# Fused attention and two MoE-style layers on one core: layer 2's weights split into two parts before they are parked in DRAM

## Chip, cores, metric

One core of one Trainium2 chip (trn2). The metric is the device time of one launch in microseconds (us). Three runs of the kernel before took 1051.81, 1053.36 and 1053.62 us: the median is 1053.36.

## What is computed

```python
def _moe_ref(x, w_in, w_out):            # layer 1
    h = x @ w_in
    g = h * np.clip(h + 3.0, 0.0, 6.0) / 6.0
    return (g @ w_out).astype(np.float32)

def _moe2_ref(x, w_in, w_out):           # layer 2
    h = x @ w_in
    sp = np.where(h > 20.0, h, np.log1p(np.exp(np.minimum(h, 20.0))))
    g = h * np.tanh(sp)
    return (g @ w_out).astype(np.float32)

attn_out = _attn_ref(q, k, v)            # 4 batches, 8 heads, 576 tokens, head size 64
x = attn_out.transpose(0, 2, 1, 3).reshape(2304, 512)
x = _moe_ref(x, moe_w_in, moe_w_out)     # 512 -> 2048 -> 512
return _moe2_ref(x, moe2_w_in, moe2_w_out)
```

Weights come as float64. The change touches only how layer 2's weights get from their float64 form to the operands of the matmuls.

## The kernel before

The 2304 tokens are cut into five blocks `j` (four of 512 columns, the last of 256), the 2048 hidden units into 16 tiles `f` of 128. One **step** is a triple (layer `m`, block `j`, tile `f`); there are 160: steps 0 to 79 are layer 1 (16 to a block, so steps 64 to 79 are its short block), steps 80 to 159 layer 2. In a step TensorE (PE) computes `ff_in` (L257 to L259: 4 x 3 matmuls of x and W_in into the PSUM tile `h`), the other engines apply the activation, and some steps later PE computes `ff_out` (L755 to L757: 4 x 3 matmuls into `y`). Three matmuls for one product, since each operand is a pair of rounded float32 tiles, an upper part and the rest: `xh`, `xl` for x, `wh`, `wl` for the weights, `gh`, `gl` for the activation. `gh` is a copy with rounding on ScalarE (ACT, L331), `gl` a subtraction on GpSimd (POOL, L338). `ff_out` of step n needs `gl` of step n at its second matmul, L756.

The order on every engine is written out by hand: for each step n, `MOE_PLAN` lists the stages in order, each with the lag in steps at which it runs. There are three plans: for layer 1's first block, for the rest of layer 1, and for layer 2. In the second plan a step issues, as far as the change and the prediction touch it: `w0` to `w3` and `whi`, `wlo` (the six pieces of a weight conversion), `in` of step n, `out` of step n - 2, `xa`, `xm`, `xh`, `xl` (the four pieces by which a tile of the next block's x is made), `c3`, `gh` and `gl` of step n - 1, `dma`, and last `a` (the first activation of step n). Engines run in their own order and wait for each other by semaphores; all these DMAs are issued on SyncE's queue (SP) in program order, and one that waits holds up those behind it.

**Conversion of layer 2's weights.** In steps 16 to 47 one half tile (128x512) a step is converted from float64 bits: `fetch2` (L145) loads the raw bits a step ahead, then `narrow` makes the float32 number: `w0` ACT `m<-raw` (L157), `w1` POOL `v<-raw` (L162), `w2` and `w3` two VectorE (DVE) operations on the bits (L165, L168). `narrow2` stores the number `v` to the DRAM tile `w2d` (L856) in the next step. In the DVE's order `w2` of step n stands ahead of `c3` of step n - 1 (L313), and POOL's `w1` of step n ahead of `gl` of step n - 1.

**x tiles in those steps.** Steps 22, 26, 28, 30 and again 38, 42, 44, 46 each also make one of the four x tiles of the next block: POOL adds two loaded parts (`xa`, L227), DVE multiplies (`xm`, L232), ACT rounds (`xh`, L239), DVE subtracts (`xl`, L244). Their loads (`load_x`, L214 to L217) are issued in steps 21, 22, 25, 28 and 37, 38, 41, 44. The part `xs` has a single buffer, so its load waits for the `xa` before.

**Loading back.** A weight tile of layer 1 is used last in its short block. `reload2` (L805) then loads `w2d[f]` into the tile `wl`, issued in step 70 + f and held until PE's `ff_out` of step 64 + f has released the tiles. Three steps later `resplit2` turns it into the pair: ACT copies it with rounding into `wh` (L810, 128x1024), then POOL and DVE each subtract one half in place (L814). These are the stages `r1` and `r2`, in steps 73 to 88; layer 2 begins at step 80.

Of the kernel before, what the change touches and what calls it, by code (L numbers as in the profile page):

```python
# [18 lines left out]
P = 128  # L19
# [6 lines left out]
FT = DFF // P  # L26
# [33 lines left out]
MOE_PLAN = (  # L60
    (
        ("c3", 1), ("gh", 1), ("gl", 1), ("w2", 0), ("w3", 0), ("w0", 0), ("xa", 0), ("w1", 0),
        ("xm", 0), ("in", 0), ("dma", 0), ("a", 0), ("out", 2), ("xh", 0), ("xl", 0), ("r2", 0),
        ("whi", 0), ("r1", 0), ("wlo", 0), ("evac", 3),
    ),
    (
        ("w0", 0), ("in", 0), ("w1", 0), ("out", 2), ("r1", 0), ("xa", 0), ("xm", 0), ("w2", 0),
        ("c3", 1), ("dma", 0), ("gh", 1), ("w3", 0), ("r2", 0), ("gl", 1), ("xh", 0), ("xl", 0),
        ("whi", 0), ("evac", 3), ("wlo", 0), ("a", 0),
    ),  # L70
    (
# [24 lines left out]
    (15.16, "gl", 0), (15.2, "conv", 3, 1, 6), (15.67, "in", 3),  # L96
)
AHEAD = 6
RELOAD = 6
RESPLIT = 3  # L100
XLOAD = (-11, -10, -7, -4), (-11, -9, -9, -6)
XSPLIT = (-10, -6, -4, -2), (-10, -8, -7, -1)
END = 0
# [2 lines left out]
def f32(ap):  # L106
    return ap.bitcast(F32)
# [7 lines left out]
def fused_kernel(ctx: ExitStack, tc: tile.TileContext, qT, kT, vv, w1, w2, outT):  # L115
    nc = tc.nc
# [6 lines left out]
    xr = ctx.enter_context(tc.tile_pool(name="xr", bufs=2))  # L123
    dpool = ctx.enter_context(tc.tile_pool(name="dpool", bufs=1, space=DRAM))
# [6 lines left out]
    x1d = dpool.tile([KT, 2, P, NT], F32, tag="x1d", name="x1d")  # L131
    rsd = dpool.tile([KT, 2, NT], F32, tag="rsd", name="rsd")
    x2d = dpool.tile([KT, P, NT], F32, tag="x2d", name="x2d")
    w2d = dpool.tile([FT, P, 1024], F32, tag="w2d", name="w2d")

    raws = {}

# [10 lines left out]
    def narrow(raw, name, x=None, tag="val", pool=False):  # L148

        low, high = raw[:, :, 0], raw[:, :, 1]  # L150
        x = x or wst.tile([P, 512], F32, tag="q", name=f"b{name}")


        if pool:
            nc.gpsimd.tensor_scalar(x, high.bitcast(F32), REBASE, 1.0, op0=ALU.mult, op1=ALU.mult)
        else:
            nc.scalar.activation(x, high.bitcast(F32), AF.Copy, scale=REBASE)  # L157
        yield

# [182 lines left out]
    with ExitStack() as late:  # L342
# [416 lines left out]
    def spare():  # L759
        return m4.tile([P, 512], F32, tag="o", name=f"m{now[0]}")  # L760
# [27 lines left out]


    conv, dmas, stores = {}, {}, {}  # L790
    xs, res = ({}, {}, {}, {}), ({}, {})

    def narrow2(n):
        for val in narrow(raws.pop((1, n)), f"2_{n}", spare(), ("q", "val")[n % 2]):
            yield
        yield
        f, c = divmod(n, 2)
        store(now[0] + 1, w2d[f, :, 512 * c:512 * c + 512], val)

    def fetch2(n):  # L800
        raws[1, n] = fetch(w2, *divmod(n, 2))

    def reload2(f):

        nc.sync.dma_start(f32(weight_tiles(1, f)[1]), w2d[f])  # L805

    def resplit2(f, t):
        hi, lo = wt[1, f]
        if t == 0:
            nc.scalar.activation(hi, f32(lo), AF.Copy)  # L810
        else:
            for c, eng in enumerate((nc.gpsimd, nc.vector)):
                cs = slice(512 * c, 512 * c + 512)
                eng.tensor_sub(lo[:, cs], f32(lo[:, cs]), f32(hi[:, cs]))  # L814

    for n, (m, j, f) in enumerate(steps):
        if m == 0 and j == 0 and f >= WMID:
            for c in range(2):
                put(conv, n - 3, weights1_spare, f, c)
                put(dmas, max(n - AHEAD, 0), fetch1, f, c, True)  # L820
        if m == 0 and 1 <= j <= 2:
            i = (j - 1) * FT + f
            put(dmas, n - 1, fetch2, i)
            put(conv, n, narrow2, i)
        if (m, j) == (0, NJ - 1):
            put(dmas, n + RELOAD, reload2, f)
            put(res[0], n + RELOAD + RESPLIT, resplit2, f, 0)
            put(res[1], n + RELOAD + RESPLIT, resplit2, f, 1)
        if f == 0 and n:
            for k in range(KT):  # L830
                put(dmas, n + XLOAD[m][k], load_x, m, j, k)
                i = n + XSPLIT[m][k]
                put(xs[0], i, add_x, m, j, k)
                put(xs[3], i, mul_x, m, j, k)
                put(xs[1], i, split_x, m, j, k, 0)
# [15 lines left out]
    def calls(*ds):  # L851
        def run_stage(n, m):
            if m == group(n):
                for d in ds:
                    for fn, *args in d.pop(n, ()):
                        fn(*args)  # L856
        return run_stage


    def conv_step(i):  # L860
        def run_stage(n, m):
            if m != group(n):
                return
            if i == 0:
                active[n] = [fn(*args) for fn, *args in conv.pop(n, ())]
            for x in active.get(n - 1 if m == 0 and i >= 2 else n, ()):
                next(x, None)
        return run_stage

    stages = dict(  # L870
        a=stage(act_a), b1=stage(act_b1), b2=stage(act_b2), ln=stage(act_ln),
        rexp=stage(act_rexp), mul=stage(act_mul), c1=stage(act_c1), c2=stage(act_c2),
        c3=stage(act_c3), gh=stage(act_gh), gl=stage(act_gl), evac=stage(evacuate),
        out=stage(ff_out), dma=calls(stores, dmas), xa=calls(xs[0]), xh=calls(xs[1]), xl=calls(xs[2]), xm=calls(xs[3]),
        r1=calls(res[0]), r2=calls(res[1]),
        w0=conv_step(0), w1=conv_step(1), w2=conv_step(2), w3=conv_step(3),
        whi=conv_step(4), wlo=conv_step(5),
    )
    stages["in"] = stage(ff_in)
    for n in range(len(steps) + 6):  # L880
        now[0] = n
        for i, plan in enumerate(MOE_PLAN):
            for name, lag in plan:
                if (name, n - lag) not in begun:
                    stages[name](n - lag, i)
    assert not (dmas or stores or conv or any(xs) or any(res))


# [37 lines left out]
```

## Time and profile before

| | us |
|---|---|
| runs, median of three | 1053.36 |
| the profiled execution's own time | 1053.55 |
| its span, first to last instruction | 1051.5 |
| PE busy | 998.3 (95%) |
| DVE busy | 647.0 (62%) |
| POOL busy | 548.8 (52%) |
| ACT busy | 515.3 (49%) |

The span is the time between the first and last instruction; 2.05 us lie around it. Busy shares are averages over stages with different limits. In the page's 40 slices (26.3 us each) PE is below nine tenths in two places, slices 9 to 12 (layer 1's start) and 25 to 28 (layer 2's start). Mean granted clock of TensorE is 0.99 of full speed.

### The profile page before, as it was taken

The page shows a single profiled execution, that of the slowest core. Times are in us where ns is not written, and L with a number is a line of the kernel's source. Part 1 is how long each engine was busy: PE and PEld are TensorE (multiplying, and loading weights), DVE is VectorE, ACT ScalarE, POOL GpSimd, SP SyncE. Part 2 cuts the span into 40 slices and gives each one's busy share as a digit, 9 for nine tenths or more (in the row PEclk, how much of TensorE's full clock was granted, in tenths as well). Part 3 has the DMA queues.
Part 4 walks back from the last instruction along what each step waited for, and adds up shares of the span by engine and source line. Part 5 has one row for each costly group of instructions (what it writes and reads, how often), then busy time and mean ns, then how long its engine had stood idle before and what let it go on. Part 6 is the DMA issues. An engine that isn't in the chain of part 4 may idle for free.

```text
span 1051.5 us, 14665 instructions
## 1 busy us (share of the span) xinstructions
PE 998.3 (95%) x5184; PEld 843.5 (80%) x5184; DVE 647.0 (62%) x1055; ACT 515.3 (49%) x1159; POOL 548.8 (52%) x494
## 2 busy tenths in 40 slices
PE   6999999988879999999999998889999999999997
PEld 5898898866557888888888996568888888888897
DVE  6888878778974444444222247996665666565664
ACT  4788888754433333333222354454444444444454
POOL 6555544567653443434222274655565555555644
PEclk9999999999999999999999999999999999999999
DMA  6677678595214755753200362000100100010010
GB/s 174 173 204 198 169 183 217 187 337 191 74 60 154 227 187 169 234 172 100 70 20 11 128 213 100 9 13 1 60 21 1 61 11 11 1 55 6 1 41 21
DMA packets 88729, 112.11 MB, mean 107 GB/s; under 512 B 41552, under 2 KB 53840, under 8 KB 88656
## 3 DMA queue, kind: packets, MB, share of 16 engines
q1 hardware_dynamic: 88656, 111.18, 34.4%
q8 instruction: 40, 0.66, 0.3%
q14 instruction: 33, 0.27, 0.1%
HBM read 74.97 MB, written 27.34 MB: 97 GB/s over the span
## 4 chain that ended last, share of the span: by engine, by line
PE 69%; POOL 8%; issue 8%; DVE 7%; ACT 4%; DMA 3%; SPq 1%; POOLq 0%; ACTq 0%; DVEq 0%
PE y L756 10%; PE y L757 10%; PE y L755 10%; PE h L259 10%; PE h L258 10%; PE h L257 10%; PE o L588 3%; POOL gl L338 3%; PE t L558 2%; PE s L485 2%; DVE v L168 2%; ACT p L518 2%; POOL wl L814 1%; DMA qb<-qs 1%; PE s L486 1%
## 5 line engine op out<-in xcount | busy, mean ns | idle before, releaser
L756 PE MATMUL y<-gl,wh 128*128 128x512 f32 (+1 forms) x640 | 238.8, 373 | 17.4 <-POOL gl L338 17.3
L257 PE MATMUL h<-xh,wh 128*128 128x512 f32 (+1 forms) x640 | 238.9, 373 | 9.7 <-ACT wh L185 6.9
L259 PE MATMUL h<-xh,wl 128*128 128x512 f32 (+1 forms) x640 | 238.3, 372 | 3.7 <-POOL wl L190 3.2
L755 PE MATMUL y<-gh,wh 128*128 128x512 f32 (+1 forms) x640 | 236.6, 370 | 2.2 <-ACT gh L331 2.2
L258 PE MATMUL h<-xl,wh 128*128 128x512 f32 (+1 forms) x640 | 237.5, 371 | 0.4 <-DVE xl L244 0.4
L757 PE MATMUL y<-gh,wl 128*128 128x512 f32 (+1 forms) x640 | 236.1, 369 | 0.0
L338 POOL TENSOR_TENSOR gl<-e,gh 128x512 fp32r<-128x512 f32 (+1 forms) x80 | 98.6, 1232 | 201.4 <-issue 93.7
L338 POOL TENSOR_TENSOR gl<-hq,gh 128x512 fp32r<-128x512 f32 (+1 forms) x80 | 125.2, 1564 | 79.9 <-ACT gh L331 79.9
L756 PEld LDWEIGHTS y<-gl,wh 128*128 128x128 f32 x640 | 121.2, 189 | 45.6 <-POOL gl L338 25.9
L257 PEld LDWEIGHTS h<-xh,wh 128*128 128x128 f32 x640 | 121.6, 190 | 33.7 <-ACT wh L185 8.6
L325 POOL TENSOR_TENSOR hq<-hq,e 128x512 f32<-128x512 f32 (+1 forms) x80 | 98.6, 1232 | 89.5 <-DVE e L306 88.9
L259 PEld LDWEIGHTS h<-xh,wl 128*128 128x128 f32 x640 | 121.7, 190 | 27.9 <-POOL wl L190 7.5
L755 PEld LDWEIGHTS y<-gh,wh 128*128 128x128 f32 x640 | 121.2, 189 | 23.1 <-ACT gh L331 2.8
L258 PEld LDWEIGHTS h<-xl,wh 128*128 128x128 f32 x640 | 121.7, 190 | 20.7 <-DVE xl L244 0.6
L757 PEld LDWEIGHTS y<-gh,wl 128*128 128x128 f32 x640 | 121.1, 189 | 19.6
L276 DVE TENSOR_SCALAR e<-e 128x512 f32<-128x512 f32 (+1 forms) x80 | 42.6, 532 | 126.0 <-ACT e L269 118.1
L269 ACT ACTIVATE e<-h 128x512 f32<-128x512 f32 (+1 forms) x80 | 44.2, 553 | 127.3 <-PE h L259 127.1
L267 ACT ACTIVATE e<-h 128x512 f32<-128x512 f32 (+1 forms) x80 | 44.0, 550 | 121.3 <-PE h L259 118.8
L313 DVE SCALAR_TENSOR_TENSOR e<-e,h 128x512 f32<-128x512 f32 (+1 forms) x80 | 50.4, 630 | 85.3 <-ACT e L267 85.2
L331 ACT ACTIVATE gh<-e 128x512 fp32r<-128x512 f32 (+1 forms) x80 | 47.0, 589 | 93.3 <-DVE e L313 93.3
L569 DVE TENSOR_TENSOR t<-t,t 128x512 fp32r<-128x512 f32 (+2 forms) x144 | 69.8, 522 | 26.9 <-ACT t L564 26.8
L288 ACT ACTIVATE e<-q 128x512 f32<-128x512 f32 (+1 forms) x80 | 47.2, 590 | 76.4 <-DVE q L283 76.4
(64 smaller groups left out, 1642.5 us busy)
## 6 DMA issues: line engine op xcount, KB each, us to landing
raw<-w SPq DMA_DIRECT2D x64, 512.0 KB
x1d<-x SPq DMA_DIRECT2D x64, 144.0 KB
qb<-qs SPq DMA_DIRECT2D x30, 288.0 KB
w2d<-v SPq DMA_DIRECT2D x32, 256.0 KB
wl<-w2d SPq DMA_DIRECT2D x16, 512.0 KB
q<-qT SPq DMA_DIRECT2D x16, 288.0 KB
k<-kT SPq DMA_DIRECT2D x16, 288.0 KB
v<-vv SPq DMA_DIRECT2D x16, 256.0 KB
```

The source lines that it names most:

```text
L257: nc.tensor.matmul(h[:, :n], hi[:, ws], xh, start=(k == 0), stop=False)
L258: nc.tensor.matmul(h[:, :n], hi[:, ws], xl, start=False, stop=False)
L259: nc.tensor.matmul(h[:, :n], lo[:, ws], xh, start=False, stop=(k == KT - 1))
L288: nc.scalar.activation(et[m, j, f], qt[m, j, f], AF.Ln, bias=2.0)
L313: nc.vector.scalar_tensor_tensor(g, g, 6.0, h, op0=ALU.min, op1=ALU.mult)
L325: nc.gpsimd.tensor_mul(g, g, et.pop((m, j, f)))
L331: nc.scalar.activation(gh, g, AF.Copy)
L338: nc.gpsimd.tensor_sub(gl, g, f32(gh))
L569: nc.vector.tensor_sub(z[:, 1, loc, :], tp, f32(z[:, 0, loc, :]))
L755: nc.tensor.matmul(y, hi[:, ws], gh, start=first, stop=False)
L756: nc.tensor.matmul(y, hi[:, ws], gl, start=False, stop=False)
L757: nc.tensor.matmul(y, lo[:, ws], gh, start=False, stop=last)
```

## The change

The conversion goes on by two pieces: after `narrow`, ACT copies the number with rounding into the buffer that held `m` (`whi`, L804 of the changed kernel), and POOL subtracts that from the number in place (`wlo`, L807). Both are stored to `w2d`, which has two parts now. In two of the 32 half tiles (steps 18 and 34) the first buffer is the x loader's `xs` tile rather than one of the four spare ones. `reload2` is issued in step 68 + f and loads both `wh` and `wl`; `resplit2` and its two stages are gone.

```diff
-RELOAD = 6
-RESPLIT = 3
+RELOAD = 4
...
-    w2d = dpool.tile([FT, P, 1024], F32, tag="w2d", name="w2d")
+    w2d = dpool.tile([FT, 2, P, 1024], F32, tag="w2d", name="w2d")
...
     def narrow2(n):
-        for val in narrow(raws.pop((1, n)), f"2_{n}", spare(), ("q", "val")[n % 2]):
+
+        f, c = divmod(n, 2)
+        dst = w2d[f, :, :, 512 * c:512 * c + 512]
+        if f % 8 == 1 and c == 0:
+
+            x = xr.tile([P, 512], F32, tag="xs", name=f"m{now[0]}", bufs=1)
+        else:
+            x = spare()
+        for val in narrow(raws.pop((1, n)), f"2_{n}", x, ("q", "val")[n % 2]):
             yield
+        nc.scalar.activation(x.bitcast(F32R), val, AF.Copy)
+        store(now[0] + 1, dst[0], x)
         yield
-        f, c = divmod(n, 2)
-        store(now[0] + 1, w2d[f, :, 512 * c:512 * c + 512], val)
+        nc.gpsimd.tensor_sub(val.bitcast(F32R), val, x)
+        store(now[0] + 1, dst[1], val)
...
     def reload2(f):
-
-        nc.sync.dma_start(f32(weight_tiles(1, f)[1]), w2d[f])
-
-    def resplit2(f, t):
-        hi, lo = wt[1, f]
-        if t == 0:
-            nc.scalar.activation(hi, f32(lo), AF.Copy)
-        else:
-            for c, eng in enumerate((nc.gpsimd, nc.vector)):
-                cs = slice(512 * c, 512 * c + 512)
-                eng.tensor_sub(lo[:, cs], f32(lo[:, cs]), f32(hi[:, cs]))
+        for part, tile in enumerate(weight_tiles(1, f)):
+            nc.sync.dma_start(f32(tile), w2d[f, part])
...
-            put(res[0], n + RELOAD + RESPLIT, resplit2, f, 0)
-            put(res[1], n + RELOAD + RESPLIT, resplit2, f, 1)
```

The order of POOL in layer 1's second block, steps 21 to 23, before. The number behind `v_` counts the half tiles (`v_5` is step 21, `v_6` step 22, which also makes an x tile), `gl_1_4` is block 1, tile 4 (step 20):

```order
L162 TENSOR_SCALAR v_5_4202<-raw 128x512
L338 TENSOR_TENSOR gl_1_4_4231<-e_1_4_4185,gh_1_4_4228 128x512
L162 TENSOR_SCALAR v_6_4250<-raw 128x512
L227 TENSOR_TENSOR xr_2_0_4221<-xr_2_0_4221,xs_2_0_4222 128x512
L338 TENSOR_TENSOR gl_1_5_4281<-e_1_5_4233,gh_1_5_4278 128x512
L162 TENSOR_SCALAR v_7_4304<-raw 128x512
L338 TENSOR_TENSOR gl_1_6_4326<-e_1_6_4287,gh_1_6_4323 128x512
```

And now, the same steps:

```order
L162 TENSOR_SCALAR v_5_4216<-raw 128x512
L338 TENSOR_TENSOR gl_1_4_4246<-e_1_4_4199,gh_1_4_4243 128x512
L807 TENSOR_TENSOR v_5_4216<-v_5_4216,m_4201 128x512
L162 TENSOR_SCALAR v_6_4267<-raw 128x512
L227 TENSOR_TENSOR xr_2_0_4236<-xr_2_0_4236,xs_2_0_4237 128x512
L338 TENSOR_TENSOR gl_1_5_4299<-e_1_5_4250,gh_1_5_4296 128x512
L807 TENSOR_TENSOR v_6_4267<-v_6_4267,m_4252 128x512
L162 TENSOR_SCALAR v_7_4324<-raw 128x512
```

One subtraction stands between the `gl` of a step and the `v` of the next.

POOL in layer 2's first block before, at tiles 3 and 4 (`wl_11` and `wl_12` are weight tiles of later steps):

```order
L325 TENSOR_TENSOR hq_0_3_6769<-hq_0_3_6769,e_0_3_6759 128x512
L814 TENSOR_TENSOR wl_11_6681<-wl_11_6681,wh_11_6680 128x512
L338 TENSOR_TENSOR gl_0_3_6863<-hq_0_3_6769,gh_0_3_6861 128x512
L325 TENSOR_TENSOR hq_0_4_6821<-hq_0_4_6821,e_0_4_6811 128x512
L814 TENSOR_TENSOR wl_12_6725<-wl_12_6725,wh_12_6724 128x512
L338 TENSOR_TENSOR gl_0_4_6913<-hq_0_4_6821,gh_0_4_6911 128x512
```

And now:

```order
L325 TENSOR_TENSOR hq_0_3_6856<-hq_0_3_6856,e_0_3_6846 128x512
L338 TENSOR_TENSOR gl_0_3_6942<-hq_0_3_6856,gh_0_3_6940 128x512
L325 TENSOR_TENSOR hq_0_4_6906<-hq_0_4_6906,e_0_4_6896 128x512
L338 TENSOR_TENSOR gl_0_4_6986<-hq_0_4_6906,gh_0_4_6984 128x512
L325 TENSOR_TENSOR hq_0_5_6948<-hq_0_5_6948,e_0_5_6938 128x512
```

The subtraction between the product `hq` and `gl` is gone; the same holds of one DVE and one ACT operation a step.

SP at the reloads before (`xr_0_0` to `xr_0_2` are x tiles of layer 2's first block):

```order
L856 DMA x2d<-o_3_3_6097 128x512
L221 DMA xr_0_0_6195<-x2d 128x512
L805 DMA wl_0_6230<-w2d 128x1024
L805 DMA wl_1_6269<-w2d 128x1024
L221 DMA xr_0_1_6271<-x2d 128x512
L221 DMA xr_0_2_6273<-x2d 128x512
L805 DMA wl_2_6308<-w2d 128x1024
```

And now:

```order
L855 DMA x2d<-o_3_3_6193 128x512
L815 DMA wh_0_6259<-w2d 128x1024
L815 DMA wl_0_6260<-w2d 128x1024
L815 DMA wh_1_6295<-w2d 128x1024
L815 DMA wl_1_6296<-w2d 128x1024
L221 DMA xr_0_0_6299<-x2d 128x512
L815 DMA wh_2_6333<-w2d 128x1024
L815 DMA wl_2_6334<-w2d 128x1024
L815 DMA wh_3_6373<-w2d 128x1024
L815 DMA wl_3_6374<-w2d 128x1024
L221 DMA xr_0_1_6377<-x2d 128x512
```

The first x tile's load stands behind four weight loads that wait for PE, where it stood ahead of all.

## Rows read from the trace of the kernel before

**Rows 1.** Table by stretch: PE, PEld, DVE, ACT, POOL busy, PEclk, DMA share, GB/s.

```profile
316.00:490.00 174.00, 172.93 (x755) 142.82 (x756) 77.07 (x114) 62.05 (x108) 72.84 (x72) 0.99 0.59 186
...
643.00:694.00 51.00, 43.05 (x173) 32.16 (x173) 48.38 (x46) 25.18 (x40) 31.84 (x22) 0.97 0.17 57
740.00:980.00 240.00, 240.00 (x1060) 198.72 (x1060) 146.16 (x239) 112.41 (x194) 140.50 (x89) 1.00 0.08 25
603.00:612.00 9.00, 9.00 (x77) 9.00 (x77) 4.48 (x7) 5.12 (x11) 4.54 (x5) 1.00 0.93 332
...
642.40:645.80 3.40, 3.11 (x7) 2.49 (x8) 3.14 (x5) 2.12 (x5) 3.09 (x3) 0.50 0.13 44
```

**Rows 2.** Waits, 643 to 694: who waited for whom, us, times, longest.

```profile
PE y L756 <- POOL gl L338: 7.7, 6, 1.5
```

**Rows 3.** Timeline of POOL, layer 2's first steps: start, us, instruction, idle before.

```profile
649.78 1.29 POOL L325 TENSOR_TENSOR hq<-hq,e 128x512 f32<-128x512 f32 x1 [2.67 <-DVE e L306]
651.03 1.74 POOL L814 TENSOR_TENSOR wl<-wl,wh 128x512 fp32r<-128x512 f32 x1
...
656.84 1.29 POOL L325 TENSOR_TENSOR hq<-hq,e 128x512 f32<-128x512 f32 x1 [2.67 <-DVE e L306]
```

**Rows 4.** Timeline of PE: first matmul of steps 83, 84, 93 and 94.

```profile
642.69 0.80 PE L257 MATMUL h<-xh,wh 128*128 128x512 f32 x1 [2.25 <-DVE e L306]
...
649.77 0.49 PE L257 MATMUL h<-xh,wh 128*128 128x512 f32 x1
...
712.63 0.39 PE L257 MATMUL h<-xh,wh 128*128 128x512 f32 x1
...
718.07 0.39 PE L257 MATMUL h<-xh,wh 128*128 128x512 f32 x1
```

**Rows 5.** Timeline of POOL, DVE and ACT, conversion step 20 and the next `v`.

```profile
340.08 0.64 POOL L162 TENSOR_SCALAR v<-raw 128x512 f32<-128x512 f32 x1
...
341.96 0.69 DVE L168 SCALAR_TENSOR_TENSOR v<-m,v 128x512 uint32<-128x512 uint32 x1
342.08 0.63 ACT L331 ACTIVATE gh<-e 128x512 fp32r<-128x512 f32 x1 [2.12 <-DVE e L313]
...
342.85 1.29 POOL L338 TENSOR_TENSOR gl<-e,gh 128x512 fp32r<-128x512 f32 x1 [2.13 <-issue]
...
344.10 0.66 POOL L162 TENSOR_SCALAR v<-raw 128x512 f32<-128x512 f32 x1
```

**Rows 6.** Source line L190, layer 1's subtraction: ns min/median/max.

```profile
L190 POOL TENSOR_TENSOR wl<-v,wh x20: 1255/1281/1294, 34.6 to 307.0; 128x512 fp32r<-128x512 f32 x20
```

**Rows 7.** Timeline of POOL: `v` of steps 22, 23, 26, 27, 28, 29.

```profile
348.61 0.64 POOL L162 TENSOR_SCALAR v<-raw 128x512 f32<-128x512 f32 x1 [0.44 <-DMA raw<-w]
...
355.84 1.08 POOL L162 TENSOR_SCALAR v<-raw 128x512 f32<-128x512 f32 x1
...
368.94 0.64 POOL L162 TENSOR_SCALAR v<-raw 128x512 f32<-128x512 f32 x1
...
378.89 0.65 POOL L162 TENSOR_SCALAR v<-raw 128x512 f32<-128x512 f32 x1 [4.04 <-PE y L756]
...
382.91 0.65 POOL L162 TENSOR_SCALAR v<-raw 128x512 f32<-128x512 f32 x1
...
388.80 1.08 POOL L162 TENSOR_SCALAR v<-raw 128x512 f32<-128x512 f32 x1
```

**Rows 8.** Timeline of SP: issue of the raw load for step 27.

```profile
373.40 0.38 SPq L145 DMA_DIRECT2D raw<-w  x1
```

**Rows 9.** Timeline of POOL: `gl` of step 16.

```profile
326.89 1.29 POOL L338 TENSOR_TENSOR gl<-e,gh 128x512 fp32r<-128x512 f32 x1 [6.22 <-issue]
```

**Rows 10.** Timeline of PE: the L756 that reads the `gl` of step 16.

```profile
332.89 0.39 PE L756 MATMUL y<-gl,wh 128*128 128x512 f32 x1
```

**Rows 11.** Source line L814, DVE's half of the resplit: ns min/median/max.

```profile
L814 DVE TENSOR_TENSOR wl<-wl,wh x16: 691/1168/1653, 608.9 to 693.1; 128x512 fp32r<-128x512 f32 x16
```

More of the change, by code (lines that the diff above doesn't have):

```diff
@@ L62 @@
         ("c3", 1), ("gh", 1), ("gl", 1), ("w2", 0), ("w3", 0), ("w0", 0), ("xa", 0), ("w1", 0),
-        ("xm", 0), ("in", 0), ("dma", 0), ("a", 0), ("out", 2), ("xh", 0), ("xl", 0), ("r2", 0),
-        ("whi", 0), ("r1", 0), ("wlo", 0), ("evac", 3),
-    ),
-    (
-        ("w0", 0), ("in", 0), ("w1", 0), ("out", 2), ("r1", 0), ("xa", 0), ("xm", 0), ("w2", 0),
-        ("c3", 1), ("dma", 0), ("gh", 1), ("w3", 0), ("r2", 0), ("gl", 1), ("xh", 0), ("xl", 0),
+        ("xm", 0), ("in", 0), ("dma", 0), ("a", 0), ("out", 2), ("xh", 0), ("xl", 0),
+        ("whi", 0), ("wlo", 0), ("evac", 3),
+    ),
+    (
+        ("w0", 0), ("in", 0), ("w1", 0), ("out", 2), ("xa", 0), ("xm", 0), ("w2", 0),
+        ("c3", 1), ("dma", 0), ("gh", 1), ("w3", 0), ("gl", 1), ("xh", 0), ("xl", 0),
         ("whi", 0), ("evac", 3), ("wlo", 0), ("a", 0),
@@ L73 @@
         ("ln", 0), ("c3", 0), ("rexp", 0), ("c1", 1), ("c2", 1), ("mul", 1), ("xa", 0), ("xm", 0),
[1 row of a table removed]
+        ("dma", 0), ("xh", 0), ("xl", 0),
     ),
@@ L790, in fused_kernel @@
     conv, dmas, stores = {}, {}, {}
-    xs, res = ({}, {}, {}, {}), ({}, {})
+    xs = {}, {}, {}, {}
     def narrow2(n):
-        for val in narrow(raws.pop((1, n)), f"2_{n}", spare(), ("q", "val")[n % 2]):
+        f, c = divmod(n, 2)
[5 more added lines that the diff above has]
+        for val in narrow(raws.pop((1, n)), f"2_{n}", x, ("q", "val")[n % 2]):
             yield
+        nc.scalar.activation(x.bitcast(F32R), val, AF.Copy)
+        store(now[0] + 1, dst[0], x)
         yield
-        f, c = divmod(n, 2)
-        store(now[0] + 1, w2d[f, :, 512 * c:512 * c + 512], val)
+        nc.gpsimd.tensor_sub(val.bitcast(F32R), val, x)
+        store(now[0] + 1, dst[1], val)
     def fetch2(n):
@@ L874, in fused_kernel @@
         out=stage(ff_out), dma=calls(stores, dmas), xa=calls(xs[0]), xh=calls(xs[1]), xl=calls(xs[2]), xm=calls(xs[3]),
-        r1=calls(res[0]), r2=calls(res[1]),
         w0=conv_step(0), w1=conv_step(1), w2=conv_step(2), w3=conv_step(3),
@@ L885, in fused_kernel @@
                     stages[name](n - lag, i)
-    assert not (dmas or stores or conv or any(xs) or any(res))
+    assert not (dmas or stores or conv or any(xs))
 def kernel(q, k, v, moe_w_in, moe_w_out, moe2_w_in, moe2_w_out):
```

1 row of the table MOE_PLAN is left out of this document.

## The prediction

> **What bounds the kernel now.** I read the table by stretch first. Where layer 2 runs undisturbed, 740 to 980, PE is busy all of the time; in the conversion steps, 316 to 490, it loses 1.1 of 174 us; in layer 2's first steps, 643 to 694, it works 43.05 of 51 us while DVE works 48.38 [rows 1]. So PE sets the pace, except where the weights are split again. The waits of that stretch say who holds PE: its L756 waits for POOL's `gl` [rows 2]. POOL's timeline says why: between the product `hq` and `gl` stands the resplit's subtraction, 1.74 us, and one `hq` comes 7.06 us after the other [rows 3]. PE's own first matmuls then price the stretch. From step 93 to 94 a step takes 718.07 - 712.63 = 5.44 us; from step 84 to 93, nine steps, 712.63 - 649.77 = 62.86 us, where PE needs 9 x 5.44 = 48.96 [rows 4]. That is 13.9 us lost. [...]
>
> The conversion steps look free, but the reader should look at POOL's ring there. From `v` of step 20 (340.08) to the next `v` (344.10) are 4.02 us, and POOL is idle for 2.13 of them, in front of `gl` [rows 5]. It is not free to work then: `v` releases DVE's `w2`, which stands ahead of `c3`, which releases ACT's `gh`, which releases `gl`, behind which stands the next `v`. This is a ring of its own, 4.02 us against PE's 5.44, and its 1.4 us to spare in plain steps pay for the slow ones.
>
> **What the change takes away.** In steps 73 to 88 one ACT copy, one POOL and one DVE subtraction a step. In layer 1's short block PE was full anyway, so nothing comes back there. In layer 2's first steps POOL's 1.74 us leave the chain, and 7.06 - 1.74 = 5.32 is below 5.44, so PE should be the bound again: 13.9 us come back. Of the 2.25 + 1.7 = 3.95 us just ahead, all or nothing may come back; the activation's chain of step 80 is needed there in any case, but an operation leaves each of three engines that it passes, so I take 2.6, nearer to all. Gain 16.5, between 13.9 and 17.9.
>
> **What it adds.** Each of the 32 half tiles gets an ACT copy, a POOL subtraction, and a second store of 256 KB. The copy can begin when the DVE's second operation has ended (341.96 + 0.69 = 342.65) and `gh` is issued; with about the 0.63 us of `gh` it ends near 343.3, before `gl` does at 344.14 [rows 5]. It is hidden by `gl`; if it were not, each step would pay up to its 0.63. The subtraction is not hidden: it stands behind `gl` and ahead of the next `v`. The same operation in layer 1 takes 1.28 us [rows 6]; as neighbours on POOL start a little early (`gl` takes 1.29, the next starts 1.25 after it), I count 1.26. **A plain step of the ring becomes 4.02 + 1.26 = 5.28 us, against PE's 5.44.** The 1.4 us to spare are 0.16 now, and the slow steps are no longer paid for.
>
> The sum over the ring, from `v` of step 17 to `v` of step 46, 29 steps:
> - 22 plain steps: 22 x 5.28 = 116.2.
> - An x step without a wait, such as 28, took 388.80 - 382.91 = 5.89, and gets 7.15. Steps 28, 30 and 44: 21.5.
> - An x step that waits for a load, such as 22, took 355.84 - 348.61 = 7.23, and gets 8.49. Steps 22 and 38: 17.0.
> - Step 26 took 378.89 - 368.94 = 9.95 [rows 7]. There SP holds an x load until POOL's `xa` of that step, and the next raw load stands behind it, issued at 373.40 [rows 8] and used 5.5 us later. The subtraction fits into POOL's wait of 4.04, but the second store stands ahead of the raw load on SP and costs one issue, 0.4. Steps 26 and 42: 20.7.
> - Now the raw load goes out only behind the stores, that is, behind the subtraction: about 0.6 us into the next step. In steps with x loads, where it takes 5.5 us, it comes 6.1 us into a step of 5.28. Steps 21, 25, 37, 41: 4 x 0.8 = 3.2. In the other steps I take it to be in time, as plain steps show no wait for it now.
>
> Sum 178.6, against 29 x 5.44 = 157.8 on PE: the ring falls back by 20.8 us. The last `gl` held, that of step 45, stands behind the x piece of step 46, another 5.89 - 4.02 = 1.9. On the other side is the ring's lead: `gl` of step 16 ends at 328.18 [rows 9] and is read at 332.89 [rows 10], 4.7; half of the first subtraction's 1.26 comes off, 4.1 stay. **PE waits 20.8 + 1.9 - 4.1 = 18.6 us for `gl` in steps 21 to 46.**
>
> One price is uncertain. DVE's half of the resplit took 0.69 us at its fastest and 1.65 at its slowest [rows 11], when POOL subtracted beside it. In plain steps the added subtraction runs while DVE waits for `v`, so it meets nothing; in x steps it meets `xl`. By rows, the step behind an x step shows up to 1.08 instead of 0.64 us for `v` [rows 7]; I take half of that, 0.2, for seven steps: 1.4. [...]
>
> Loss 20.0, bounds 9 (the ring's plain and x steps alone: 22 x 5.28 + 7 x 7.15 = 166.2, 8.4 over PE, plus 1.9, minus the lead, and some 3 for the two held steps) and 27 (below).
>
> **Moved, and costed at nothing.** The reloads are issued two steps earlier, but each waits for PE to release its tiles, so they go out when they did, twice as many. A pair is 1.05 MB; the fastest comparable stretch moved 332 GB/s [rows 1], so a pair takes 3.2 us in a short step of at least 2.7: some 0.5 us of backlog a step, 7 us after 14, and layer 2 uses one pair in 5.44 us from some 40 us later on. Behind the first four weight loads on SP now stands layer 2's first x tile; ACT's rounding of it may wait, and `a` of that step behind it. The cover is the lead of `gl` in the short block; without it, up to 3 us. The second store's issue on SP is covered by SP's wait for the subtraction. The `xs` tile in two steps spares ACT a wait for x2d's store in a step with lead: nothing.
>
> **Sum:** 20.0 - 16.5 = +3.5. The profiled execution took 1053.55 us (0.19 over the median of the runs): 1057.0.
>
> **The rivals.**
> - *The loads are not late (faster).* The place is the raw load of steps 21, 25, 26 and their like. At 4.2 us instead of 5.5 (an estimate: in plain steps the load goes out about half a microsecond behind 342.65 and is used by the `v` after next, near 348.1, without a wait, so it took under 5 [rows 5]) the held steps lose 1.3 each, the loading steps nothing, and if `xl` costs nothing either the loss is 20.0 - 2.6 - 3.2 - 1.4 = 12.8: 1053.55 - 3.7 = 1049.8. It decides from a loss under 16.5, a raw load near 4.4 us. For it: in plain steps `v` follows `gl` with no wait. Against: steps 22 and 27 did wait [rows 7].
> - *The loads are late in plain steps too.* The second store's 0.26 MB take 0.8 us at 332 GB/s, mostly ahead of the raw load. At 0.6 + 4.2 + 0.8 = 5.6 a plain step pays 0.3, 22 of them 7: loss 27, time 1064.
> - *Layer 2's start gives back less:* the wait ahead of step 84 stays, recovery takes some steps, the first x tiles hold ACT: gain 11 to 12, time 1062.
> - *The subtraction hides in POOL's 2.13 us of idle time:* loss 0, time 1037. Against it is POOL's order: it stands behind `gl`, not ahead of it.
>
> **How the numbers follow.** Forecast 0.47 (1053 to 1060.5), loads early 0.22, late 0.15, less given back 0.10, hidden 0.06. A difference of 0.2%, 2.1 us, is what a measurement of this kernel can tell from none: faster means under 1051.25, slower over 1055.47. Faster: most of the second case and the last, 0.23. Same: the low end of the forecast, 0.17, and 0.05 of the second, 0.22. Slower: the rest, 0.55. The range 1048 to 1066 leaves out the last case, a tip of the second and the upper ends of the late ones, under 2 in 10.
>
> **What would show it.** In the conversion steps: `v` to `v` 5.3 us in plain steps, 7 to 8.5 in x steps, 10 in 26 and 42; PE's L756 waiting for `gl` L338 by some 20 us where it waited hardly at all. In layer 2's first steps: PE at 5.44 us a step from step 84 on, no such wait. Wrong it would be if PE stays full between 316 and 490, or if steps 84 to 93 stay well over 49 us.

## The result and the profile after

The changed kernel takes 1060.88 us (median of 4 runs, 1059.59 to 1062.09); the kernel before, beside it, 1053.44. The ratio is 1.0074, 95% interval 1.0056 to 1.0091: slower by 7.4 us where 3.5 were forecast, inside the range. The profiled execution took 1061.40 us, its span is 1059.3.

First the busy times of the page, after:

```profile
span 1059.3 us, 14759 instructions
...
PE 1001.9 (95%) x5184; PEld 846.1 (80%) x5184; DVE 611.4 (58%) x1039; ACT 519.7 (49%) x1175; POOL 567.1 (54%) x510
```

POOL works 18 us more, DVE 36 us less, PE 3.6 us more: what changed is above all where PE waits. The table by stretch of the changed kernel (columns as in [rows 1]) shows the first of the two places, and that the second has healed:

```profile
316.00:490.00 174.00, 163.00 (x684) 131.11 (x684) 65.92 (x97) 69.44 (x120) 96.81 (x88) 0.97 0.63 207
600.00:650.00 50.00, 50.00 (x379) 48.24 (x378) 11.61 (x23) 17.01 (x40) 12.94 (x16) 1.00 0.73 282
665.00:716.00 51.00, 50.05 (x219) 41.14 (x220) 34.77 (x55) 25.72 (x45) 31.18 (x20) 1.00 0.16 53
740.00:980.00 240.00, 240.00 (x1060) 198.72 (x1060) 145.53 (x237) 112.67 (x195) 140.47 (x89) 1.00 0.08 25
```

In the conversion steps PE works 163.0 of 174 us where it had worked 172.93 [rows 1]. The reloads, 600 to 650, cost PE nothing. The row from 665 holds the steps that stood at 643 to 694 before: 50.05 of 51 us instead of 43.05. What ended PE's waits in the conversion steps (316 to 520; us, times, longest), now and before:

```profile
PE y L755 <- ACT gh L331: 7.6, 4, 3.1
PE y L756 <- POOL gl L338: 5.1, 6, 0.9
PE y L755 <- ACT o L781: 4.5, 1, 4.5
```

```profile
PE y L755 <- ACT gh L331: 1.8, 1, 1.8
PE y L756 <- POOL gl L338: 0.8, 1, 0.8
```

Here `o` is the copy by which ACT and DVE empty a finished PSUM tile `y`.

How much PE lost and got back is read from PE's first matmuls, those of steps 49, 84 and 93 after, and of step 49 before:

```profile
522.87 0.39 PE L257 MATMUL h<-xh,wh 128*128 128x512 f32 x1
...
671.83 0.39 PE L257 MATMUL h<-xh,wh 128*128 128x512 f32 x1
...
720.79 0.39 PE L257 MATMUL h<-xh,wh 128*128 128x512 f32 x1
```

```profile
498.59 0.39 PE L257 MATMUL h<-xh,wh 128*128 128x512 f32 x1
```

By step 49 PE is 522.87 - 498.59 = 24.3 us late. From 49 to 84 it takes 148.96 us instead of 649.77 - 498.59 = 151.18 [rows 4], 2.2 less; from 84 to 93 it takes 48.96 us, exactly 9 x 5.44, instead of 62.86, 13.9 less. So 24.3 lost, 16.1 given back, 8.2 net; the spans differ by 7.8, so 0.4 us come back elsewhere.

POOL's timeline in the conversion steps answers to [rows 5] and [rows 7] (start, us, instruction, idle before):

```profile
344.10 1.30 POOL L338 TENSOR_TENSOR gl<-e,gh 128x512 fp32r<-128x512 f32 x1 [2.13 <-issue]
345.36 1.30 POOL L807 TENSOR_TENSOR v<-v,m 128x512 fp32r<-128x512 f32 x1
346.62 0.65 POOL L162 TENSOR_SCALAR v<-raw 128x512 f32<-128x512 f32 x1
...
359.68 1.74 POOL L807 TENSOR_TENSOR v<-v,m 128x512 fp32r<-128x512 f32 x1
361.38 0.65 POOL L162 TENSOR_SCALAR v<-raw 128x512 f32<-128x512 f32 x1
...
377.25 0.65 POOL L162 TENSOR_SCALAR v<-raw 128x512 f32<-128x512 f32 x1
377.86 1.28 POOL L227 TENSOR_TENSOR xr<-xr,xs 128x512 f32<-128x512 f32 x1
381.87 1.27 POOL L338 TENSOR_TENSOR gl<-e,gh 128x512 fp32r<-128x512 f32 x1 [2.73 <-issue]
383.11 1.73 POOL L807 TENSOR_TENSOR v<-v,m 128x512 fp32r<-128x512 f32 x1
388.44 0.64 POOL L162 TENSOR_SCALAR v<-raw 128x512 f32<-128x512 f32 x1 [3.60 <-DMA raw<-w]
```

The subtraction stands between `gl` and the next `v`, 1.30 us, as the prediction drew it; beside an x tile it takes 1.74; and in the held step 26, 377.25 to 388.44 = 11.19 us, `v` waits for the raw load. SP's timeline says when that load went out:

```profile
381.09 0.53 SPq L855 DMA_DIRECT2D w2d<-m  x1
381.66 0.43 SPq L855 DMA_DIRECT2D w2d<-v  x1
382.14 0.51 SPq L145 DMA_DIRECT2D raw<-w  x1
```

### The profile page after: what moved, and what is told of

Read it like the earlier page. It is cut to its first block, busy times and chain, and to the rows that moved or that the text cites. A ratio compares the mean times of both kernels' runs of the same rounds, so it can differ in the third digit from the quotient of the medians.

```text
span 1059.3 us, 14759 instructions
## 1 busy us (share of the span) xinstructions
PE 1001.9 (95%) x5184; PEld 846.1 (80%) x5184; DVE 611.4 (58%) x1039; ACT 519.7 (49%) x1175; POOL 567.1 (54%) x510
## 4 chain that ended last, share of the span: by engine, by line
PE 46%; issue 3%; POOL 3%; ACT 1%; DVE 0%; POOLq 0%; DVEq 0%
PE y L756 8%; PE y L757 8%; PE y L755 8%; PE h L258 7%; PE h L259 7%; PE h L257 7%; POOL gl L338 1%; POOL hq L325 1%; ACT gh L331 1%; POOL xr L227 0%; POOLq L919 0%; DVE q L283 0%; DVE hq L318 0%; DVE e L300 0%; ACT e L269 0%
## 5 line engine op out<-in xcount | busy, mean ns | idle before, releaser
L756 PE MATMUL y<-gl,wh 128*128 128x512 f32 (+1 forms) x640 | 241.1, 377 | 12.0 <-POOL gl L338 12.0
L755 PE MATMUL y<-gh,wh 128*128 128x512 f32 (+1 forms) x640 | 239.6, 374 | 12.5 <-ACT gh L331 7.9
L338 POOL TENSOR_TENSOR gl<-hq,gh 128x512 fp32r<-128x512 f32 (+1 forms) x80 | 127.6, 1595 | 89.7 <-ACT gh L331 88.9
L756 PEld LDWEIGHTS y<-gl,wh 128*128 128x128 f32 x640 | 122.3, 191 | 40.3 <-POOL gl L338 20.3
L755 PEld LDWEIGHTS y<-gh,wh 128*128 128x128 f32 x640 | 122.3, 191 | 36.0 <-ACT gh L331 10.5
L258 PEld LDWEIGHTS h<-xl,wh 128*128 128x128 f32 x640 | 121.3, 190 | 20.7 <-DVE xl L244 0.6
L276 DVE TENSOR_SCALAR e<-e 128x512 f32<-128x512 f32 (+1 forms) x80 | 33.2, 415 | 144.6 <-ACT e L269 136.6
L269 ACT ACTIVATE e<-h 128x512 f32<-128x512 f32 (+1 forms) x80 | 44.5, 556 | 144.7 <-PE h L259 144.7
L165 DVE SCALAR_TENSOR_TENSOR v<-raw,v 128x512 uint32<-128x512 uint32 x64 | 43.9, 701 | 78.5 <-POOL v L162 78.5
L518 ACT ACTIVATE p<-s,nm 128x64 f32<-128x64 f32 (+2 forms) x144 | 75.2, 531 | 14.4 <-DVE nm L507 14.4
```

What stands on the lines that cost most here:

```text
L258: nc.tensor.matmul(h[:, :n], hi[:, ws], xl, start=False, stop=False)
L338: nc.gpsimd.tensor_sub(gl, g, f32(gh))
L518: nc.scalar.activation(t, sc, AF.Exp, bias=nm[:, c:c + 1], accum_out=su[:, i:i + 1])
L755: nc.tensor.matmul(y, hi[:, ws], gh, start=first, stop=False)
L756: nc.tensor.matmul(y, hi[:, ws], gl, start=False, stop=False)
```

## The experiments

The question was what the 24.3 us are made of: POOL's longer ring, the doubled stores, ACT's copy, or PE's own idle stretches. All ratios are to the kernel before on the same chip.

**The subtraction on DVE.**

```diff
-        nc.gpsimd.tensor_sub(val.bitcast(F32R), val, x)
+        nc.vector.tensor_sub(val.bitcast(F32R), val, x)
```

> The changed kernel with one edit: the subtraction of the low part in the conversion steps is done by DVE instead of POOL; copy, both stores and both loads stay. Theory (POOL's ring: gl, subtraction, next v): the subtraction leaves the ring, v to v in plain steps falls from 5.28 back to about 4.0 us, PE's 5.44 us a step set the pace again, and nearly all of the 24.3 us that PE lost by step 49 come back, while layer 2's start keeps its gain of 16.1: 1053.4 - 16.1 = 1037 to 1041 us. Rival 1 (traffic: the doubled stores and the loads behind them make the raw loads late): the held steps 26 and 42 keep their 11.2 and 12.7 us and 10 or more of the 24.3 us stay: 1047 us or more. Rival 2 (the ACT copy, not the subtraction, is what holds the step): no change, 1060.9.

Measured: 1050.26 us, ratio 0.9981 (0.9971 to 0.9992). Some 10 us better than the change, yet 10 short of the theory. Of the 22 plain steps 7 did fall to 4.0 to 4.2 us; POOL's waits (316 to 500) and two places in its and SP's timeline show what held most of the others:

```profile
POOL v L162 <- DMA raw<-w: 29.8, 13, 6.8
```

```profile
350.84 0.66 POOL L162 TENSOR_SCALAR v<-raw 128x512 f32<-128x512 f32 x1 [1.16 <-DMA raw<-w]
...
387.34 0.64 POOL L162 TENSOR_SCALAR v<-raw 128x512 f32<-128x512 f32 x1 [6.65 <-DMA raw<-w]
```

```profile
345.78 0.32 SPq L855 DMA_DIRECT2D w2d<-v  x1
346.21 0.37 SPq L145 DMA_DIRECT2D raw<-w  x1
...
382.23 0.49 SPq L145 DMA_DIRECT2D raw<-w  x1
```

The raw load goes out behind the store of the low part and is used 4.6 to 5.1 us later; in 13 steps `v` waited for it. The held steps 26 and 42 took 12.58 and 12.69 us, and the time is in the first rival's range: by this run alone the cause could be the traffic or the order on SP. The first theory, one ring, fell. Theory 2: there are **two rings side by side**, POOL's and that of the raw loads behind the stores on SP, and the longer one counts. With the subtraction on POOL the first is longer in plain steps and hides the second.

**The second split left out** (of the kernel before).

```diff
-RELOAD = 6
+RELOAD = 4
...
-        nc.sync.dma_start(f32(weight_tiles(1, f)[1]), w2d[f])
+        for tile in weight_tiles(1, f):
+            nc.sync.dma_start(f32(tile), w2d[f])
...
-            put(res[0], n + RELOAD + RESPLIT, resplit2, f, 0)
-            put(res[1], n + RELOAD + RESPLIT, resplit2, f, 1)
```

> The kernel before without its second split (the copy and both subtractions in steps 73 to 88 are left out, and both tiles of a weight are loaded from the one stored tensor, so layer 2 works with weights that are not split); the conversion steps are those of the kernel before. Theory (gain and loss are two separate things): the gain alone, layer 2's steps 84 to 93 at 5.44 us each: 1053.4 - 16.1 = 1037.3 us, 1036 to 1039. Rival (the doubled loads of the short block are in time in the changed kernel only because PE comes there 24 us late): PE waits for weights in the first steps of layer 2, 1040 us or more.

Measured: 1037.24 us, ratio 0.9856 (0.9841 to 0.9872); span 1035.4 against 1051.5, 16.1 us less. That is the gain alone, and the doubled loads, issued as early as in the change, are in time even where PE is not late.

**Both splits** (the changed conversion steps in the kernel before).

```diff
...
+        nc.scalar.activation(x.bitcast(F32R), val, AF.Copy)
+        store(now[0] + 1, dst[0], x)
         yield
-        f, c = divmod(n, 2)
-        store(now[0] + 1, w2d[f, :, 512 * c:512 * c + 512], val)
+        nc.gpsimd.tensor_sub(val.bitcast(F32R), val, x)
+        store(now[0] + 1, dst[1], val)
...
-        nc.sync.dma_start(f32(weight_tiles(1, f)[1]), w2d[f])
+        nc.sync.dma_start(f32(weight_tiles(1, f)[1]), w2d[f, 1])
```

> The changed kernel's conversion steps (copy, subtraction on POOL, two stores) with the kernel before's second split: only the low parts are loaded back, and they are split again, so layer 2 works with the low parts alone. The loss without the gain. Theory (loss and gain are separate, 24.3 us lost by step 49, 16 given back in layer 2's first steps): 24 us over the kernel before, 22 to 26, near 1076 us. Rival (a part of what PE loses in the conversion steps would have been lost in layer 2's first steps in any case, so that gain and loss are not separate): under 20 us over the kernel before.

Measured: 1077.64 us, ratio 1.0231 (1.0213 to 1.0249), 24.3 us of 1053: the loss alone. Layer 2's first steps keep their old wait; from 640 to 740 this row is the same in both kernels, 9.8 us (7.7 in the shorter stretch of [rows 2]):

```profile
PE y L756 <- POOL gl L338: 9.8, 8, 1.5
```

Loss and gain are separate, and their sum, 24.3 - 15.2 = 9.1 us by these two ratios, lies near the change's 7.8 by its own.

**The y tiles emptied earlier.** Two edits of the order in the conversion steps of the changed kernel: ahead of ACT's copy, and at the head of the step.

```diff
-        ("whi", 0), ("evac", 3), ("wlo", 0), ("a", 0),
+        ("evac", 3), ("whi", 0), ("wlo", 0), ("a", 0),
```

> The changed kernel with one edit: in the conversion steps ACT and DVE empty the finished y tiles ahead of the ACT copy of the weights instead of behind it. In the changed kernel PE stands 4.53 us in step 34 behind that emptying, and its granted clock is 0.5 for 3.4 us after it. Theory (the ring sets the end of the stretch, PE's own idle time only takes the place of a later wait for gl): the idle time at L755 goes, the waits for gl in steps 36 to 46 grow by nearly as much, and only the ring's step from 35 to 36, 7.06 us, becomes 5.28: 1059 us, 1058 to 1060.5. Rival (the losses add up): 4.5 us and half of 3.4 come back, 1054.7 us.

Measured: 1061.01 us, ratio 1.0084 (1.0066 to 1.0102). Nothing moved, but PE's wait was not gone either:

```profile
PE y L755 <- ACT gh L331: 9.2, 5, 4.0
PE y L756 <- POOL gl L338: 5.4, 6, 0.9
PE y L755 <- ACT o L781: 4.0, 1, 4.0
```

On DVE the emptying stands behind the step's second operation on the bits, which the late ring holds. So this run could not tell, and the second edit followed:

```diff
-        ("w0", 0), ("in", 0), ("w1", 0), ("out", 2), ("xa", 0), ("xm", 0), ("w2", 0),
+        ("evac", 3), ("w0", 0), ("in", 0), ("w1", 0), ("out", 2), ("xa", 0), ("xm", 0), ("w2", 0),
...
-        ("whi", 0), ("evac", 3), ("wlo", 0), ("a", 0),
+        ("whi", 0), ("wlo", 0), ("a", 0),
```

> The changed kernel with one edit: in the conversion steps ACT and DVE empty the finished y tiles at the head of the step, ahead of the step's conversion work, since putting it ahead of ACT's copy alone left 4.00 of PE's 4.53 us of idle time: DVE's part had stood behind the step's second operation on the bits. Theory (the rings set the end of the stretch): the idle time at L755 behind o falls under 1 us, PE waits for gl later instead, and only the step of v from 35 to 36, 7.06 us, falls back to 5.3: 1 to 2 us less, 1058 to 1060. Rival (PE's losses add up): 4.5 us and half of the 3.4 us at granted clock 0.5 come back, 1054 to 1055.5 us.

Measured: 1060.74 us, ratio 1.0080 (1.0062 to 1.0098). The wait for `o` is gone, and PE's first matmuls of steps 36 and 49 show what became of it:

```profile
436.08 0.39 PE L257 MATMUL h<-xh,wh 128*128 128x512 f32 x1
...
521.52 0.39 PE L257 MATMUL h<-xh,wh 128*128 128x512 f32 x1
```

In the changed kernel itself step 36 begins here:

```profile
443.60 0.39 PE L257 MATMUL h<-xh,wh 128*128 128x512 f32 x1
```

PE is 7.5 us earlier at step 36 and 1.35 at step 49. It waits for `gh` and `gl` instead; 1.35 us do not show in the runs. PE's longest single wait was worth next to nothing, since the rings set the end of the stretch. The expected 5.3 us for `v` from 35 to 36 did not come either (6.84): that delay is not PE's. In the changed kernel the raw load of that step stands on SP behind four stores of `o` and goes out 1.14 us into the step instead of 0.48. In this run it goes out at 0.48 and is used 6.36 us later, where the two raw loads before, in the changed kernel, are used 4.77 and 4.75 us later (425.17 to 429.94, 430.43 to 435.18). With loads first (below) step 35 takes 5.28, but step 36 takes 6.34 then. The cause of this delay stays open.

**The x loads earlier** (of the changed kernel; in the two blocks with conversions the first load one step earlier, the second tile split two steps earlier).

```diff
-                put(dmas, n + XLOAD[m][k], load_x, m, j, k)
-                i = n + XSPLIT[m][k]
+                mid = n in (32, 48)
+                put(dmas, n + (-12, -10, -7, -4)[k] if mid else n + XLOAD[m][k], load_x, m, j, k)
+                i = n + ((-10, -8, -4, -2)[k] if mid else XSPLIT[m][k])
```

> The changed kernel with one edit: in the two blocks with conversions the x tiles' first load is issued one step earlier, and the second tile is split two steps earlier, so that SP no longer holds the third tile's load (and the raw load behind it) until POOL has added the second. Theory (ring, with SP's hold as the cause of the 11.19 and 12.71 us in steps 26 and 42): these two steps become plain, 5.28 us; steps 24 and 40 become x steps of 7.57; steps 22 and 38 fall from 9.2 to 7.6: 13.3 - 4.6 + 3.3 = 12 us less, 1049 us; 1052 if steps 22 and 38 keep their wait. Rival (the loads are slow because of the doubled traffic, wherever SP issues them): the wait for the raw load moves to another step, under 4 us come back, 1057 us or more.

Measured: 1050.75 us, ratio 0.9986 (0.9977 to 0.9996), 9 us less than the change by the two ratios, where 12 were expected; by its span, 1047.5 us, it is 11.8. The held steps 26 and 42 fell from 11.19 and 12.71 to 5.58 and 5.68 us. SP's hold was their cause.

**Loads ahead of stores, with the subtraction on DVE.**

```diff
-        out=stage(ff_out), dma=calls(stores, dmas), xa=calls(xs[0]),
+        out=stage(ff_out), dma=calls(dmas, stores), xa=calls(xs[0]),
```

> The kernel with the subtraction on DVE, and one more edit: in each step SP issues the loads ahead of the stores, where before it issued them behind. Theory 2 (formed from the run with the subtraction on DVE: the raw load of the next step stands on SP behind the store of the low part, lands 4.6 to 5.2 us after its issue, and so sets the pace of every second step once POOL's ring is short): the load goes out most of a step earlier, the waits of v for raw go except in the steps where SP holds an x load, 26 and 42, which fall from 12.6 to about 10, as in the kernel before; PE then loses at most 2 us by step 49: 1036 to 1040 us. Rival (the doubled stores slow the loads as traffic, wherever they are issued): v goes on waiting for raw in every second step, 1047 us or more.

Measured: 1038.31 us, ratio 0.9871 (0.9855 to 0.9886). The same bytes move, and by the two ratios 11.6 us are gone: it was the order on SP, not the traffic. SP's timeline has the raw load of step 22, 3.85 us earlier than above, and POOL's its `v`, now 7.1 us behind and without a wait:

```profile
342.36 0.33 SPq L145 DMA_DIRECT2D raw<-w  x1
```

```profile
349.43 1.09 POOL L162 TENSOR_SCALAR v<-raw 128x512 f32<-128x512 f32 x1
```

A miss in the detail: the held steps were to fall to about 10 us, and took 11.80 and 11.29; the other steps are shorter than PE's 5.44 us on average now and pay for them.

**The x loads earlier, with the subtraction on DVE.**

> The kernel with the subtraction on DVE, with the x tiles' loads and splits moved as in the run with the x loads earlier; stores stay ahead of loads. Theory 2: the held steps 26 and 42 (12.6 and 12.7 us) are gone, and what stays is the raw load behind the store, about 5.1 us a step on average against PE's 5.44, more beside x loads: 10 to 12 us less than with DVE alone, 1038 to 1041 us. Rival (the hold only collects lateness that shows anywhere): the waits move to the neighbouring steps, 1045 us or more.

Measured: 1041.79 us, ratio 0.9911 (0.9895 to 0.9927): 7.4 us less than with DVE alone, where theory 2 gave 10 to 12. The held waits of 6.65 and 6.76 us are down to 0.97 and 1.78, but `v` still waits for raw, in 18 steps by 26.3 us in all where it was 29.8. So outside the held steps the waits grew by some 7 us: as the rival had it, most of the waiting moved to other steps. Each wait is 3.4 us at most now, and the time did not stay at the rival's 1045; that the slack of those steps covers the rest is likely and was not shown.

**All three edits.**

> All three edits: subtraction on DVE, loads ahead of stores, x loads and splits moved. Theory 2: neither ring is longer than PE's 5.44 us, PE is full from 316 to 490, and only the gain in layer 2 is left: 1036 to 1038 us, as with the second split left out. Rival (traffic or contention of DVE's subtraction beside POOL's work keep the stretch slow): 1042 us or more.

Measured: 1037.74 us, ratio 0.9862 (0.9848 to 0.9876), the same as without any second split. The conversion steps are full again, with the changed kernel's whole work in them, and PE waits 0.8 us there (316 to 520):

```profile
316.00:490.00 174.00, 173.27 (x756) 143.02 (x757) 112.61 (x145) 79.24 (x137) 81.33 (x72) 0.99 0.68 230
```

```profile
PE y L756 <- POOL gl L338: 0.8, 1, 0.8
```

This beats both kernels, by 1.4% and by 2.1%.

**Loads ahead of stores, with the subtraction on POOL.**

> The changed kernel with one edit: SP issues a step's loads ahead of its stores; the subtraction stays on POOL. Theory 2 (two rings; with the subtraction on POOL the raw load is late only where SP holds an x load): plain steps stay 5.28 us, x steps 7.57, the held steps 26 and 42 fall from 11.2 and 12.7 to about 10.3: some 3 to 4 us less, 1056 to 1058 us. Rival (the load behind the stores is the whole loss, POOL's subtraction none of it): 1040 us.

Measured: 1056.72 us, ratio 1.0039 (1.0024 to 1.0054), as theory 2 has it: of the order on SP only some 4 us show while POOL's ring is the longer. The held steps took 11.51 and 11.38 us, not 10.3, so of these two only step 42 gained (1.3); most of the saving lay in steps 22 and 38, 7.58 and 7.59 us instead of 9.47 and 9.03. Step 35 takes 5.28 instead of 7.06, but step 36 takes 6.34 instead of 5.29.

**All but DVE.**

> The changed kernel with loads ahead of stores and with the x loads and splits moved, the subtraction still on POOL: neither SP's holds nor the stores delay a raw load any more, so what is left is the price of POOL's subtraction in its ring. Theory (ring: 22 plain steps of 5.28 and 7 x steps of 7.57 between v of 17 and v of 46, 169.2 us against 157.8 on PE, plus the x piece of step 46, less the lead of 4): PE loses 10 to 12 us by step 49, 1048 to 1050.5 us, 11 to 13 over the same kernel with the subtraction on DVE. Rival (most of POOL's price was the late loads): 1042 us or less.

Measured: 1048.50 us, ratio 0.9958 (0.9944 to 0.9971), by the ratios 10.1 us over the same kernel with the subtraction on DVE, a little under the 11 to 13 expected. POOL no longer waits for any load in this stretch; PE works this much of it:

```profile
316.00:490.00 174.00, 166.45 (x712) 134.84 (x713) 72.01 (x106) 73.14 (x130) 105.18 (x96) 0.98 0.66 218
```

The eight kernels with the change, as ratios to the kernel before:

| x loads | SP's order | subtraction on POOL | on DVE | POOL's price, us |
|---|---|---|---|---|
| as changed | stores first | 1.0074 | 0.9981 | 9.8 |
| as changed | loads first | 1.0039 | 0.9871 | 17.7 |
| earlier | stores first | 0.9986 | 0.9911 | 7.9 |
| earlier | loads first | 0.9958 | 0.9862 | 10.1 |

The price is the difference times 1053.4. Read by rows or by columns, no edit has a price of its own: loads first is worth 3.7 us on POOL and 11.6 on DVE, and the x loads, with loads first, 8.5 on POOL and 0.9 on DVE. The ratios' intervals reach 1 to 2 us to either side, so 7.9, 9.8 and 10.1 cannot be told apart, nor 0.9 from nothing; 17.7 and the 3.7 against 11.6 stand clear of that. All three edits together take back 22.3 us by the ratios, nearly all of the 24.3; ACT's copy and the second stores stay in that kernel, and it is as fast as the one without them.

## Why the prediction was right, and where its sizes were off

The mechanism came as drawn: a longer ring of POOL in the conversion steps, and PE as the bound again in layer 2's first steps. The time, 1061, lies just above the forecast's own 1053 to 1060.5, toward the case of the late loads. The sum was a small difference of two large terms, so 4.3 us too little in one of them and 0.4 too much in the other made 8.2 out of 3.5.

- *Layer 2's first steps, 16.5 predicted:* 16.1. Steps 84 to 93 gave the 13.9 to the hundredth; just ahead 2.2 came back instead of 2.6. Step 83 waits 1.26 us where it had 2.25, and the granted clock behind it is 1.00 where it had been 0.50 [rows 1]. No run shows the 1.7 of the sum's 2.25 + 1.7 by itself: it is half of the 3.4 us at granted clock 0.50 [rows 1], an estimate. In the kernel before, the first seven matmuls of step 83 take 645.83 - 642.69 = 3.14 us; at the 5.44 / 24 = 0.227 of an undisturbed step they would take 1.59, so 1.55 us are lost there.
- *Plain steps of the ring, 5.28:* 5.24 to 5.30 in 18 of 22. The order `gl`, subtraction, `v` was the whole reason, and the table's last row shows the price of POOL's ring by itself: 10.1 us.
- *The loss, 20.0 predicted, 24.3 measured, was the mis-sized term.* From `v` of step 17 (323.67) to `v` of step 46 (508.52) the ring took 184.85 us, where 178.6 and 1.4 for contention were predicted: 4.85 more. By kind of step (the third and fourth nearly cancel, which is luck):
  - steps 26 and 42: 11.19 + 12.71 instead of 20.7 + 0.4, 2.8 more. The second store did cost the 0.4 us counted for it: the raw load goes out 382.14 - 377.25 = 4.89 us into the step, before 373.40 - 368.94 = 4.46 [rows 7, 8]. But it is used 6.3 us later instead of 5.5, and in step 42 7.8 us later; the prediction took the load's own time as fixed. It goes out among twice as many stores now, but that they slow it was not tried by itself.
  - x steps: 7.59, 7.56, 7.59 and, with a wait, 9.47 and 9.03, 1.7 more in all. The contention is not 0.2 but 0.45 us a step (1.74 against 1.29), in every one of them.
  - steps 21, 25, 37 and 41: 3.2 us for a late raw load were predicted, and none came; they took 5.27 to 5.29.
  - plain steps: 3.5 more in all, not foreseen: 1.8 in steps 17 to 19 (5.83, 6.10 and 5.72; the first two took 8.10 and 7.90 us in the kernel before already) and 1.8 in step 35 (7.06).
- *The rest of the loss:* the x piece of step 46 took 7.56 - 5.28 = 2.3 instead of 1.9, and with these the lead comes out, as what is left over, at 184.85 - 157.8 + 2.3 - 24.3 = 5.1 instead of 4.1. Read as in [rows 9] and [rows 10], `gl` of step 16 ends at 328.29 and is read at 332.99, 4.7 as before: half a subtraction did not come off.
- *Where PE waits came out otherwise.* L756 was to wait some 20 us for `gl`; it waits 5.1 (0.8 before), and L755 waits 7.6 for `gh` and 4.5 for `o`. PE is late by what the ring lost, but it meets the late ring at other places too.
- *PE's own stops were not foreseen:* the wait of 4.53 us for `o`, and three drops of the granted clock to 0.50 or 0.51 behind PE's waits (of 2.41, 4.53 and 3.09 us); the last row is the stretch behind the 1.26 us of step 83, at 1.00:

```profile
393.40:396.80 3.40, 3.40 (x10) 2.62 (x9) 1.17 (x2) 0.00 (x0) 2.19 (x3) 0.51 0.63 165
434.40:437.80 3.40, 3.40 (x10) 2.62 (x9) 1.89 (x3) 1.53 (x4) 1.43 (x2) 0.50 1.02 381
492.40:499.20 6.80, 5.49 (x12) 4.03 (x13) 2.19 (x4) 2.27 (x4) 4.38 (x4) 0.50 0.47 141
665.60:669.00 3.40, 3.24 (x13) 2.36 (x13) 3.33 (x6) 1.90 (x4) 2.58 (x2) 1.00 0.64 196
```

  At the lower clock PE was busy for 3.40 + 3.40 + 5.49 us. Its matmuls start 0.43 us apart there (435.86, 436.29), and 0.23 at full clock (438.14, 438.37), so by estimate some 6 us of its lateness stand there and not in a wait. That they are missing from the sum did no harm, as the run with the tiles emptied at the head of the step shows for the wait for `o` and the drop behind it: the sum was made over the ring, and PE behind it has time to give away.
- *The rivals.* Loads not late: true of the four loading steps, but not of the held ones, and the time did not follow. (Its estimate of a load under 5 us leaned on a `v` near 348.1 without a wait; the row has it at 348.61 with a wait of 0.44 [rows 7].) Loads late in plain steps too: they were once the subtraction had left POOL, `v` of step 20 by 1.8 us, and `v` of step 36, which had waited 2.3 in the kernel before, by 3.8; with the subtraction on POOL its ring hid nearly all of it. The prediction had one ring with late loads added to it; there were two, and it counted late loads where the other ring covered them, 3.2 us. Layer 2's start gives back less: no. The subtraction hides in POOL's idle time: no, that idle time stands ahead of `gl` and stayed, 2.13 us.
- *Costed at nothing, and rightly:* ACT's copy (with the copy in place, all three edits give the time without it) and the reloads.

## What to carry to other kernels

Idle time of an engine is not room (POOL's 2.13 us ahead of `gl` stayed, and a plain step of its ring went from 4.02 to 5.28 us): ask where in the ring of who-waits-for-whom the added operation stands, and whether a free place on another engine lies off that ring. Where two rings run side by side, taking time off the longer one only shows the other (with the subtraction on DVE 9.8 of the 24.3 us came back, with all three edits 22.3), so price edits in pairs before giving one up. On a queue that issues in order, as SP's does here, put the loads that somebody waits for ahead of stores that wait for somebody: with the x loads as changed that was worth 11.6 us with the subtraction on DVE and 3.7 with it on POOL.

## What the runs showed of the hardware

DVE's subtraction and POOL's operations beside it stood in each other's way: the later one ended, but for 0.13 us, as if it had waited for the earlier, and the earlier one was not slowed. With the subtraction on DVE, DVE's timeline and POOL's around step 20:

```profile
344.41 1.35 DVE L807 TENSOR_TENSOR v<-v,m 128x512 fp32r<-128x512 f32 x1 [0.70 <-ACT m L804]
```

```profile
343.91 1.30 POOL L338 TENSOR_TENSOR gl<-e,gh 128x512 fp32r<-128x512 f32 x1 [2.12 <-issue]
345.17 1.10 POOL L162 TENSOR_SCALAR v<-raw 128x512 f32<-128x512 f32 x1
```

DVE's subtraction took 0.68 us at its fastest. Here it starts within `gl`, which ends at 345.21, and 345.21 + 0.68 = 345.89 against its end at 345.76; POOL's `v`, 0.65 us alone, starts within the subtraction, and 345.76 + 0.65 = 346.41 against its end at 346.27. So each ends about 0.13 us before it would if it had waited for the other's end to begin. This holds all through the conversion steps of that run: 29 of DVE's 32 subtractions start within a POOL operation, and every one ends 0.13 or 0.14 us before that sum, whether it took 0.90 or 1.36 us; the other three take 0.68 or 0.69. The one that came first is not slowed: `gl` takes 1.27 to 1.31 us with or without it. In the changed kernel the same sum gives the contention of an x step: POOL's subtraction starts at 359.68, within DVE's `xl`, which runs from 358.84 for 1.42 us, to 360.26, and 360.26 + 1.29 = 361.55 less 0.13 is the subtraction's end at 361.42.

```profile
358.84 1.42 DVE L244 TENSOR_TENSOR xl<-xr,xh 128x512 fp32r<-128x512 f32 x1 [0.62 <-ACT xh L239]
```

In the kernel before, DVE's half of the resplit took its 1.65 us not for POOL's subtraction but where it began within POOL's product `hq`, which ends at 649.78 + 1.29 = 651.07 [rows 3]; 651.07 + 0.69 less 0.13 is 651.63, and it ends at 651.62:

```profile
649.97 1.65 DVE L814 TENSOR_TENSOR wl<-wl,wh 128x512 fp32r<-128x512 f32 x1 [0.27 <-ACT wh L810]
```
